# Signs of a gate group moved to the next even pair, its counts to the next odd one, and the last six row tiles reordered over two value buffers

## Chip, cores and metric

One core of a Trainium2 chip runs the kernel. The metric is the time of one execution on the device in microseconds (us), lower being better. Engines work in parallel, each on its own instructions in order: TensorE (PE; PEld is its weight load), VectorE (DVE), ScalarE (ACT), GpSimd (POOL) and SyncE (SP), which issues nearly all DMA transfers. Matrix products land in PSUM; everything else lies in SBUF.

## What is computed

Chunked attention, then a mixture of experts over its output. The reference, cut:

```python
# q, k, v: (8, 8, 576, 64); chunks of 64 rows
scores = scale * q_c @ k_c.T;  scores -= max(scores)
attn = exp(scores) / (sum(exp(scores)) + 1e-9)
x = (attn @ v_c)  ->  (4608, 512)
logits = x @ w_gate                       # 8 experts
expert_idx = argmax(logits);  probs = softmax(logits)
for e in range(8):                        # capacity 80
    tok = rows of expert e, the 80 with the largest gate weight if more
    out[tok] = gate_w[tok] * (relu(x[tok] @ w1[e]) @ w2[e])
```

Rows that no expert keeps are zero in the output. w1 and w2 of one expert are 2 MB each in float32.

## The kernel before

The 4608 rows are 36 row tiles of 128, worked in 18 pairs (loop at line 659). Pair n is spread over time: in iteration n TensorE computes `scores(n)`, transposes the probabilities of pair n-1 (`probs`, line 335), multiplies with the values of pair n-2 (`values`, tiles 2n-4 and 2n-3, line 355) and transposes the finished x of pair n-3 (`xtrans`, line 396). VectorE takes maxima, subtracts them (`minus`) and divides the values by their sums (`divide`, line 373). ScalarE takes the exponential of the transposed scores and copies transposed x out of PSUM. The values of a row tile go to one PSUM buffer, tag "o"; scores have another of the same size, tag "s", transposes a third, "tp". SP loads q, k and v, three pairs ahead, and stores x.

Four row tiles make a gate group T. In the odd ("due") pair 2T+5 `gate_mm` multiplies transposed x by w_gate, `gate_copy` brings the logits to SBUF and `gate_sum` transposes them back. `gate` (line 426) then puts a chain of small steps into the queue `gates`: maximum, shift, exponential, sum, one-hot of the best expert, a level from 1 to 256 made of the bits of the gate weight (`lb`, `bb`, `bo`), its inverse and the key with its three bf16 parts. `fill` takes the next step from the queue; the calls of `fill` are spread over the loop by hand and so set the place of each step. For rows below 32 the arithmetic of the level is on GpSimd.

The last queued steps are `count` and `left_add`. `count` has ScalarE compute, for each of the four row tiles, the sign of the level against 1 to 256 (`signs`, line 511); `left_add` has TensorE sum these per expert (`tally`, line 521) and VectorE subtract them from `left`, the capacity left at each level. With 14 queued steps before it, `count` comes up two pairs later, in the next odd pair, behind `gate_copy`, and `tally` before the values of the second tile:

```python
if rt < 28:
    queue.append((left_add, (rt, n)))
```

Behind the loop (line 704) the last row tiles are written out by hand: the probabilities of the last pair in two halves (`probs_last`), values 32 to 35, the last transposes and gate groups 7 and 8. `threshold` (line 551) finds each expert's smallest kept level. Rows above it are numbered, compacted with one-hot matrices (`hot`) and gathered. Weights of experts 0 and 1 come early, in eight parts (`early_weights`, from pair 15 on); parts 6 and 7 wait, through a small copy on GpSimd, for the last keyed levels `kb`. Behind them SP clears the first five of nine blocks of `out` and then loads the weights of experts 2 to 7 (line 863) as their buffers come free. The experts run six blocks of 128 slots on TensorE (`layer1`, line 183; `layer2`, line 215); the second block needs expert 2.

## Time and profile before

| | us |
|---|---|
| median of 3 runs | 288.51 |
| their range | 284.03 to 291.04 |
| the profiled execution | 285.64 |
| its span on the page | 283.8 |
| PE busy | 232.1 (82%) |
| PEld busy | 142.4 (50%) |
| DVE busy | 118.8 (42%) |
| ACT busy | 69.0 (24%) |
| POOL busy | 49.2 (17%) |
| DMA, mean rate | 299 GB/s of 84.80 MB |

Busy times are shares of the whole span; they average over stages that have different limits. A timeline row gives start, length, engine, line, operation, output from input, and in brackets the idle time just before and what ended it. "issue" is idle time for which the profile shows no cause.

### The profile page before, as it was taken

The numbers are of one execution on the slowest core, as the hardware profiler recorded it, in microseconds if no ns is written. First come the engines' busy times: TensorE is split into PE (matmuls) and PEld (weight loads), VectorE is DVE, ScalarE is ACT, GpSimd is POOL, SyncE is SP. The second block draws the span as 40 slices with busy tenths as digits, with TensorE's granted clock in tenths as the row PEclk, the third lists the DMA queues.
The fourth block names the chain that finished last, engine by engine and source line by source line (L and its number), as shares of the span: only waits on it lengthen the run. The fifth ranks groups of instructions, "written<-read, shape, count | busy, mean of one in ns | idle before, by whom it ended". The sixth has DMA issues, their size and how long they took to land. (4 is left out here: it accounts for less than half of the span.)

```text
span 283.8 us, 8481 instructions
## 1 busy us (share of the span) xinstructions
PE 232.1 (82%) x3697; PEld 142.4 (50%) x3697; DVE 118.8 (42%) x305; ACT 69.0 (24%) x120; POOL 49.2 (17%) x153
## 2 busy tenths in 40 slices
PE   8677888784889789785786794939999999999990
PEld 5556777673767677674564581303333332423320
DVE  4565778581656758384354872000020111111010
ACT  1121432524352434435243501102020010201000
POOL 5030003040221313040222737000000011010011
PEclk9797999998797979799689997977999999999997
DMA  7989999988497898476798599999999999992001
GB/s 267 381 272 389 345 352 383 349 267 302 128 329 245 276 309 271 139 275 247 233 290 285 185 362 411 413 415 393 410 406 402 413 404 407 413 404 112 3 35 32
DMA packets 35194, 84.80 MB, mean 299 GB/s; under 512 B 3472, under 2 KB 3600, under 8 KB 35152
## 3 DMA queue, kind: packets, MB, share of 16 engines
q1 hardware_dynamic: 33904, 80.72, 78.7%
q0 software_dynamic: 960, 2.88, 2.6%
q8 instruction: 31, 0.51, 0.7%
q10 hardware_dynamic: 288, 0.59, 0.5%
q14 instruction: 11, 0.09, 0.1%
HBM read 64.00 MB, written 20.45 MB: 298 GB/s over the span
## 5 line engine op out<-in xcount | busy, mean ns | idle before, releaser
L366 PE MATMUL o<-vb,pT 128*64 128x130 f32 x576 | 44.8, 301 | 11.4 <-issue 6.2
L190 PE MATMUL hc<-w,xtc 128*32 128x512 f32 x384 | 47.7, 632 | 4.5 <-DMA w<-in_w 4.4
L366 PEld LDWEIGHTS o<-vb,pT 128*64 128x64 f32 x576 | 35.4, 148 | 14.7 <-issue 8.7
L223 PE MATMUL yc<-w,htc 128*32 128x512 f32 x384 | 42.3, 592 | 0.0
L303 PE MATMUL s<-qk 64*64 64x64 f32 x1152 | 24.9, 239 | 6.3 <-issue 4.6
L190 PEld LDWEIGHTS hc<-w,xtc 128*32 128x32 f32 x384 | 12.4, 115 | 34.2 <-issue 28.4
L314 DVE TENSOR_REDUCE mx<-s 128x16 f32<-128x1024 f32 (+1 forms) x19 | 22.2, 1166 | 15.2 <-PE s L303 15.1
L340 ACT ACTIVATE pT<-pt 128x1024 f32<-128x1024 f32 x17 | 17.4, 1024 | 40.2 <-PE pt L331 40.2
L223 PEld LDWEIGHTS yc<-w,htc 128*32 128x32 f32 x384 | 12.4, 110 | 28.3 <-issue 28.3
L303 PEld LDWEIGHTS s<-qk 64*64 64x64 f32 x1152 | 21.8, 150 | 9.4 <-issue 6.3
L379 DVE TENSOR_TENSOR x<-o,rc 128x512 f32<-128x512 f32 x36 | 24.9, 691 | 1.2
L406 ACT COPY xT<-px 128x1024 f32<-128x1024 f32 x17 | 17.2, 1012 | 33.3 <-PE px L331 33.3
L229 POOL DMA_INDIRECT out<-ysc,si x6 | 6.0, 996 | 95.5 <-issue 49.7
L321 DVE TENSOR_TENSOR sm<-s,mx 128x1024 f32<-128x1024 f32 (+1 forms) x19 | 22.1, 1161 | 0.1
L195 ACT ACTIVATE hsc<-hc 128x512 f32<-128x512 f32 x6 | 3.6, 599 | 71.9 <-PE hc L190 71.9
L228 DVE TENSOR_SCALAR ysc<-yc,gatec 128x512 f32<-128x512 f32 x6 | 4.5, 751 | 33.0 <-PE yc L223 33.0
L212 DVE COPY htc<-hpc 128x512 f32<-128x512 f32 x6 | 4.2, 692 | 29.9 <-PE hpc L208 29.9
L490 POOL TENSOR_SCALAR u<-sx 128x4 f32<-128x4 f32 x8 | 1.6, 195 | 83.6 <-DVE sx L489 75.1
L538 PE MATMUL ph<-mine,lv 128*128 128x8 bf16 x72 | 7.1, 173 | 10.4 <-ACT lv L513 10.3
L331 PE MATMUL px<-ct,x 64*128 64x64 f32 x288 | 14.7, 251 | 0.9 <-ACT xT L406 0.9
L331 PEld LDWEIGHTS px<-ct,x 64*128 64x128 f32 x288 | 11.9, 158 | 4.7 <-issue 3.6
L197 DVE TENSOR_SCALAR hsc<-hc 128x512 f32<-128x512 f32 x6 | 4.2, 692 | 23.7 <-PE hc L190 23.7
(132 smaller groups left out, 235.5 us busy)
## 6 DMA issues: line engine op xcount, KB each, us to landing
w<-in_w SPq DMA_DIRECT2D x12, 2048.0 KB, 20.6
qk<-in_qk SPq DMA_DIRECT2D x35, 512.0 KB, 6.1
vb<-in_vv SPq DMA_DIRECT2D x72, 130.0 KB, 5.3
out<-zero SPq DMA_DIRECT2D x9, 1024.0 KB, 15.0
xs<-x SPq DMA_DIRECT2D x16, 512.0 KB, 5.8
w<-in_w SPq DMA_DIRECT2D x8, 1024.0 KB, 7.2
xs<-x SPq DMA_DIRECT2D x4, 256.0 KB, 4.2
qk<-in_qk ACTq DMA_DIRECT2D x1, 512.0 KB, 5.3
```

Source lines behind the costliest of these rows:

```text
L190: nc.tensor.matmul(h[o:o + 32, :], lhsT=xT[r][:, b, o:o + 32], rhs=getw(groups[r][g])[0][:, b, 512 * f:512 * f + 512], start=(b == 0), sto ...
L223: nc.tensor.matmul(y[o:o + 32, :], lhsT=hT[r][c // 4][:, c % 4, o:o + 32], rhs=getw(groups[r][g])[1][:, c, :], start=(c == 0), stop=(c == ...
L229: nc.gpsimd.indirect_dma_start(out=out, out_offset=bass.IndirectOffsetOnAxis(ap=si[:, r:r + 1], axis=0), in_=ys, in_offset=None, bounds_ch ...
L303: nc.tensor.matmul(ps[64 * u:64 * u + 64, h, c:c + 64], lhsT=t8[64 * h:64 * h + 64, 0, pr, u, :], rhs=t8[64 * h:64 * h + 64, 1, pr, u, :], ...
L314: nc.vector.tensor_reduce(d['mx'][:, :, c0:c1], d['s8'][:, :, c0:c1], axis=AX.X, op=ALU.max)
L321: nc.vector.tensor_tensor(d['sm'][:, c0:c1].rearrange("p c k h -> p h c k"), d['s8'][:, :, c0:c1], d['mx'][:, :, c0:c1, None].to_broadcast ...
L331: nc.tensor.transpose(pm[:, u, 64 * c:64 * c + 64], src(c)[rows], ident[rows, rows])
L340: nc.scalar.activation(d['pT'], pt, AF.Exp, scale=0.125)
L366: nc.tensor.matmul(po[64 * u:64 * u + 64, pr // 2, o:o + 130].rearrange("p (h x) -> p h x", h=2), lhsT=d['pT'][:, u, c:c + 64], rhs=v[:, : ...
L379: nc.vector.tensor_tensor(TT[T][:, r, :].rearrange("p (j m e) -> p j m e", j=2, m=4), pov[..., 0:64], rc[:, :, :, None].to_broadcast([P, 2 ...
L406: nc.scalar.copy(dst, pm)
L538: nc.tensor.matmul(ph[:, b, :], lhsT=U['lv', j][0][:, P * b:P * b + P], rhs=mine[:, j, :], start=not ab and rt != 24 and j == rt, stop=j = ...
```

## The change

- In the loop, the counts are no longer queued. In even pairs from 6 on the queue is emptied behind `xtrans`, and the four `signs` of the last group follow there. In odd pairs `tally` of the group before stands right behind `gate_copy`, and `left_add` (now the addition alone) behind the first divide. `gate_sum` comes behind the store of the pair instead of before `minus`; seven `fill`s follow instead of five.
- The chain is cut in three: `chain` to the level, `rest` (keyed level, sum plus 1e-9) and `late` (inverse, key). For the last three groups only `chain` is queued and the other parts are called by name; the keys are always GpSimd's.
- The counts of rows 24 to 27 come from comparisons on GpSimd (`steps_`), with a sum over the own rows 0 to 23 taken at the end of pair 16.
- The loop breaks off in the last pair. The last six row tiles follow in a new order, their values alternating between buffers "o" and "s"; maxima, subtraction and probabilities of the last pair are no longer in halves; the last x transpose uses "o", and the last gate takes the first pair's half first.
- Early weights 6 and 7 wait for the levels `bo`; 4 warming matmuls stand where 16 stood. Gate buffers are three deep instead of two.

```diff
         def gate_mm(T):
             pl = U['pl', T] = ps2.tile([P, P], F32, name=f"L{T}", tag="g")
-            for pr in range(4):
-                for j in range(4):
-                    xt = XT[2 * T + j // 2].rearrange("p c u j -> p c (u j)")
-                    nc.tensor.matmul(
-                        pl[32 * j:32 * j + 32], lhsT=wgp[:, pr], rhs=xt[:, 4 * (j % 2) + pr, :],
-                        start=pr == 0, stop=pr == 3, tile_position=(0, 32 * j))
+            order = [(pr, j) for pr in range(4) for j in range(4)]
+            if T == LG:
+                order.sort(key=lambda x: x[1] // 2)
+            for pr, j in order:
+                xt = XT[2 * T + j // 2].rearrange("p c u j -> p c (u j)")
+                nc.tensor.matmul(
+                    pl[32 * j:32 * j + 32], lhsT=wgp[:, pr], rhs=xt[:, 4 * (j % 2) + pr, :],
+                    start=pr == 0, stop=pr == 3, tile_position=(0, 32 * j))
...
             def key():
-                p.tensor_tensor(kk, oh, g[:, :, None].to_broadcast(bc), op=ALU.mult)
-                if rt >= 32:
-                    S['parts'] = parts
-                else:
-                    parts()
+                nc.gpsimd.tensor_tensor(kk, oh, g[:, :, None].to_broadcast(bc), op=ALU.mult)
+                parts()
...
-            def count():
-                if rt < 32:
-                    for j in range(rt, rt + n):
-                        signs(j)
-                else:
-                    signs(rt)
-                    for j in range(rt + 1, rt + n):
-                        steps_(nc.vector, j)
-
-            for fn in (
+            chain = [
                     lambda: v.tensor_reduce(m, lg, axis=AX.X, op=ALU.max),
                     shifted,
                     first,
@@ -492,21 +468,24 @@
                                             op=ALU.is_equal),
                     lambda: p.tensor_scalar(lb, u8.bitcast(I32), SHIFT, LOW + 1.0,
                                             op0=ALU.mult, op1=ALU.max),
-                    lambda: p.tensor_scalar(g, sx, 1e-9, None, op0=ALU.add),
                     level,
-                    lambda: v.reciprocal(g, g),
-                    lambda: p.tensor_scalar(bo[:, sl], bb, 2.0 ** -10, None, op0=ALU.add),
+                    lambda: p.tensor_scalar(bo[:, sl], bb, 2.0 ** -10, None, op0=ALU.add)]
+            rest = [
                     lambda: p.tensor_tensor(kb[:, :, sl].rearrange("p e r -> p r e"), oh,
                                             bb[:, :, None].to_broadcast(bc),
                                             op=ALU.mult),
-                    key,
-                    count):
-                if fn is count and rt == 28:
-                    S['signs'] = count
-                else:
-                    queue.append((fn, ()))
-            if rt < 28:
-                queue.append((left_add, (rt, n)))
+                    lambda: (v if rt == 24 else nc.gpsimd).tensor_scalar(
+                        g, sx, 1e-9, None, op0=ALU.add)]
+            late = [lambda: v.reciprocal(g, g), key]
+            for fn in chain + ([] if rt >= 24 else rest + late):
+                queue.append((fn, ()))
+            S['counts'] = [(signs, (j,)) for j in range(rt, rt + n)]
+            S["level", rt], S["sum", rt] = rest
+            S["inverse", rt], S["key", rt] = late
+
+        def rest(rt, *what):
+            for w in what:
+                S.pop((w, rt))()
...
-            if rt == 24:
-                cnt = gk.tile([P, NE], BF16, name="cnt", tag="cnt", bufs=1)
-                with nc.allow_low_precision(reason="whole numbers up to 28"):
-                    nc.vector.tensor_reduce(cnt, mine[:, 0:28, :].rearrange("p r e -> p e r"),
-                                            axis=AX.X, op=ALU.add)
             for b in range(2):
                 if rt == 24:
-                    nc.tensor.matmul(ph[:, b, :], lhsT=ones_b, rhs=cnt, start=True, stop=False)
...
-        def left_add(rt, n):
-            tally(rt, n)
+        def own_counts():
+            cnt = S['cnt'] = gk.tile([P, NE], BF16, name="cnt", tag="cnt", bufs=1)
+            with nc.allow_low_precision(reason="whole numbers up to 24"):
+                nc.vector.tensor_reduce(cnt, mine[:, 0:24, :].rearrange("p r e -> p e r"),
+                                        axis=AX.X, op=ALU.add)
+
+        def left_add(rt):
             if S.setdefault('first', rt) == rt:
                 nc.vector.tensor_scalar(left, U['ph', rt], -0.5, capt, op0=ALU.mult, op1=ALU.add)
...
+            rest(32, "level")
             with nc.allow_low_precision(reason="whole numbers up to 256"):
                 nc.vector.tensor_scalar(thr, pn, 1.0, None, op0=ALU.max)
...
                 if due:
                     gate_mm(T)
                     gate_copy(T)
-                maxima(n, 0, 4 if last else 8)
+                    if T >= 1:
+                        tally(4 * T - 4, 4)
+                maxima(n)
+                if last:
+                    minus(n)
+                    divide(2 * (n - 2))
+                    left_add(4 * T - 4)
+                    break
                 fill()
                 if n + NB < NPAIR:
                     for t in range(2):
                         load_qk(2 * (n + NB) + t)
                 if n >= 2:
                     divide(2 * (n - 2))
+                    if due and T >= 1:
+                        left_add(4 * T - 4)
                     fill()
                     values(2 * (n - 2) + 1)
                     if n - 2 + NBV // 2 < NPAIR:
                         load_v(2 * (n - 2) + 1 + NBV)
                 if n >= 3:
                     xtrans(n - 3)
-                if due:
-                    gate_sum(T, gates)
-                minus(n, 0, 4 if last else 8)
+                if n >= 6 and not due:
+                    flush(gates)
+                    for fn, args in S['counts']:
+                        fn(*args)
+                minus(n)
                 fill()
-                if last:
-                    maxima(n, 4, 8)
-                    minus(n, 4, 8)
                 if n >= 2:
                     divide(2 * (n - 2) + 1)
                     store(n - 2)
-                for j in range(5):
+                if due:
+                    gate_sum(T, gates)
+                for j in range(7):
                     fill()
+                if n == NPAIR - 2:
+                    own_counts()
                 for k in EARLY.get(n, ()):
                     early_weights(k)
-            n = NPAIR - 1
-            values(2 * n - 2)
-            probs_last(n, 0)
-            divide(2 * n - 2)
-            fill()
-            fill()
-            probs_last(n, 1)
-            values(2 * n - 1)
-            xtrans(n - 2)
-            divide(2 * n - 1)
-            store(n - 1)
-            for k in EARLY[NPAIR]:
+
+            def pops(k):
+                for j in range(k):
+                    fill()
+            values(31, "s")
+            probs(17)
+            gate_sum(6, gates)
+            values(32)
+            divide(31)
+            store(15)
+            for k in EARLY[17]:
                 early_weights(k)
-            values(2 * n)
+            pops(3)
+            values(33, "s")
+            xtrans(14)
+            divide(32)
+            pops(2)
+            values(34)
+            divide(33)
+            store(16)
+            for k in EARLY[18]:
+                early_weights(k)
             flush(gates)
-            values(2 * n + 1, "s")
+            for j in range(24, 28):
+                steps_(nc.gpsimd, j)
+            xtrans(15)
+            values(35, "s")
+            divide(34)
             gate_mm(7)
             gate_copy(7)
-            divide(2 * n)
-            xtrans(n - 1)
-            divide(2 * n + 1)
-            store(n)
-            for k in EARLY[NPAIR + 1]:
+            xtrans(16)
+            divide(35)
+            store(17)
+            for k in EARLY[19]:
                 early_weights(k)
             gate_sum(7, gates)
-            xtrans(n)
+            pops(2)
+            xtrans(17, "o")
             gate_mm(8)
+            flush(gates)
             gate_copy(8)
+            rest(24, "sum", "inverse")
+            signs(28)
+            signs(29)
+            gate_sum(8, gates)
+            tally(24, 4)
+            keep_warm(4)
+            pops(2)
+            rest(24, "level", "key")
+            signs(30)
+            signs(31)
+            left_add(24)
             flush(gates)
-            gate_sum(8, gates)
-            keep_warm(16)
-            fill()
-            fill()
-            S.pop('signs')()
+            signs(32)
+            for j in range(33, 36):
+                steps_(nc.vector, j)
             for k in (6, 7):
-                early_weights(k, kb[:, 0, 28 + 3 * (k - 6):29 + 3 * (k - 6)])
-            flush(gates)
-            S.pop('parts')()
+                early_weights(k, bo[:, 28 + 4 * (k - 6):29 + 4 * (k - 6)])
+            tally(28, 4)
+            left_add(28)
+            tally(32, 4)
+            rest(28, "level", "sum")
+            rest(32, "sum")
+            rest(28, "inverse", "key")
+            rest(32, "inverse", "key")
             for k in range(3):
                 clear(k)
-            left_add(28, 4)
-            tally(32, 4)
             keep_warm(1)
             threshold()
```

`maxima` and `minus` lose their column arguments, `halves` and `xtrans` gain a `tag`, `probs_last` goes, and the small gate tiles get `bufs=3`. `LG` is the last group, 8. `steps_` and `signs` are unchanged.

## Rows read from the trace of the kernel before

**Rows 1.** Windows by stage: length, engines' busy time, granted clock, DMA share, GB/s
```profile
34.00:39.95 5.95, 5.95 (x166) 4.97 (x162) 3.93 (x6) 2.40 (x4) 0.00 (x0) 1.00 0.95 316
46.63:125.03 78.40, 62.85 (x1490) 52.25 (x1486) 48.77 (x121) 30.64 (x50) 15.72 (x70) 0.89 0.79 262
125.03:158.45 33.42, 24.11 (x416) 18.72 (x413) 15.68 (x62) 13.38 (x27) 8.83 (x41) 0.90 0.76 258
158.45:174.44 15.99, 11.16 (x129) 8.70 (x127) 11.11 (x50) 2.33 (x8) 8.76 (x10) 0.99 0.95 345
174.44:189.59 15.15, 10.63 (x77) 3.36 (x77) 1.00 (x3) 1.88 (x4) 2.00 (x2) 0.84 1.04 414
189.59:283.80 94.21, 86.87 (x764) 29.39 (x764) 12.12 (x17) 8.73 (x15) 5.98 (x6) 0.95 0.76 297
```

**Rows 2.** Timeline, SP's clears and TensorE's wait for expert 2
```profile
158.75 10.07 SPq L593 DMA_DIRECT2D out<-zero  x5
...
189.59 6.06 PE L190 MATMUL hc<-w,xtc 128*32 128x512 f32 x28 [4.43 <-DMA w<-in_w]
```

**Rows 3.** Windows, first odd pair, sum of five odd, then of five even pairs
```profile
46.63:54.90 8.27, 6.82 (x174) 5.50 (x170) 4.25 (x8) 4.00 (x8) 1.71 (x8) 1.00 1.00 353
...
sum 48.22, PE 38.29 PEld 30.83 DVE 21.11 ACT 20.80 POOL 8.56; mean PE 7.66 PEld 6.17 DVE 4.22 ACT 4.16 POOL 1.71
...
sum 30.18, PE 24.56 PEld 21.42 DVE 27.66 ACT 9.84 POOL 7.16; mean PE 4.91 PEld 4.28 DVE 5.53 ACT 1.97 POOL 1.43
```

**Rows 4.** Timeline of one odd pair, from its scores to its second values
```profile
79.53 1.16 PE L303 MATMUL s<-qk 64*64 64x64 f32 x64
...
82.31 1.08 PE L413 MATMUL L<-xT,wgp 128*32 128x128 f32 x32
...
83.62 1.70 ACT L513 ACTIVATE lv<-io_b,bo 128x256 bf16<-128x256 bf16 x4
...
84.18 0.18 PE L538 MATMUL ph<-mine,lv 128*128 128x8 bf16 x1 [0.79 <-ACT lv L513]
...
85.38 0.29 PE L538 MATMUL ph<-mine,lv 128*128 128x8 bf16 x5 [0.22 <-ACT lv L513]
...
85.60 2.00 PE L366 MATMUL o<-vb,pT 128*64 128x130 f32 x16
```

**Rows 5.** Groups by line, ScalarE and VectorE: busy us, mean ns, idle before
```profile
L340 ACT ACTIVATE pT<-pt 128x1024 f32<-128x1024 f32 x17 | 17.4, 1024 | 40.2 <-PE pt L331 40.2
L406 ACT COPY xT<-px 128x1024 f32<-128x1024 f32 x17 | 17.2, 1012 | 33.3 <-PE px L331 33.3
...
L379 DVE TENSOR_TENSOR x<-o,rc 128x512 f32<-128x512 f32 x36 | 24.9, 691 | 1.2
L314 DVE TENSOR_REDUCE mx<-s 128x16 f32<-128x1024 f32 x17 | 20.8, 1223 | 14.7 <-PE s L303 14.6
L321 DVE TENSOR_TENSOR sm<-s,mx 128x1024 f32<-128x1024 f32 x17 | 20.7, 1217 | 0.1
L378 DVE RECIPROCAL rc<-rc 128x8 f32<-128x8 f32 x36 | 7.3, 203 | 1.2
L377 DVE TENSOR_SCALAR rc<-o 128x8 f32<-128x8 f32 x36 | 5.7, 160 | 7.0 <-PE o L366 6.4
```

**Rows 6.** Groups by line, GpSimd
```profile
L578 POOL TENSOR_SCALAR pk<-ct,ptok 128x128 bf16<-128x128 f32 x2 | 2.9, 1444 | 0.9 <-ACT ptok L770 0.9
...
L498 POOL TENSOR_SCALAR bo<-bb 128x4 f32<-128x4 bf16 x8 | 1.8, 230 | 0.7
```

**Rows 7.** Timeline, the last logits' transpose and the threshold
```profile
153.47 0.33 PE L423 MATMUL lT<-ct,lt 128*128 128x128 f32 x1 [0.37 <-ACT lt L419]
...
158.45 0.17 DVE L559 TENSOR_SCALAR thr<-pn 128x8 bf16<-128x8 f32 x1 [0.28 <-PE pn L557]
```

**Rows 8.** A stall of TensorE in the timeline, and the page's instruction queue
```profile
66.77 1.08 PE L413 MATMUL L<-xT,wgp 128*32 128x128 f32 x31 [2.73 <-issue]
...
q8 instruction: 31, 0.51, 0.7%
```

48 lines of the change are left out of this document (18 added, 30 removed).

## The prediction

> **What bounds the kernel now.** I read the stages first [rows 1]. From 189.59 us to the end TensorE is busy for 86.87 of 94.21 us while DMA has room (share 0.76), so that stage is a fixed tail. It can begin only when expert 2's first weight matrix has landed: TensorE waits 4.43 us for it at 189.59 [rows 2]. Ahead of that matrix in SP's queue stand five clears, issued from 158.75 on [rows 2]. DMA is full between the clears and the landing (share 0.95, then 1.04, 414 GB/s) [rows 1]. So the end follows when the clears are issued, and with them the last two early weights, which wait for the last gate values. That time is set by the attention loop and by the stretch behind its last pair, and there DMA has room: share 0.79 over ten pairs and 0.76 behind [rows 1].
>
> Inside the loop I compared the two kinds of pair [rows 3]. Five odd pairs, which hold a gate group, take 48.22 us together (9.64 each); five even ones take 30.18 (6.04 each). The timeline of one odd pair shows why [rows 4]: the gate matmuls run from 82.31 to 83.39, then TensorE waits for ScalarE's four signs (0.79 us before the first count matmul, then 0.22 before each), and the next values start only at 85.60, 2.21 us behind the gate. They then take 2.00 us; over the ten pairs the granted clock is 0.89 of full speed, against 1.00 in the pair at 34.00, which has a gate group but no counts yet [rows 1]. That pair takes 5.95 us. It is the nearest row there is for an odd pair whose counts find their signs ready.
>
> **The change part by part.** *Signs moved.* They leave the odd pair, where they stand behind the copy of the gate logits on ScalarE, and go behind the copy of x transposed in the even pair before. Four take 1.70 us [rows 4]. Behind them on ScalarE waits only the next pair's exponential. In an even pair ScalarE does one exponential (1.02), one copy (1.01) [rows 5] and now 1.70, together 3.7 of 6.04 us. The signs end about 2.7 us behind the start of their copy, and the next exponential has its input about 2.9 us behind the next scores (2.78 for scores, values and transpose up to the gate [rows 4]). So they hide, with little to spare; uncovered they would cost up to 1.7 us a pair. The level is ready by then: the flush in front of the signs only pulls forward small steps that GpSimd does at 0.23 us each [rows 6]. VectorE's reciprocal waits for six of these in a row, some 1.8 us, and VectorE is in the maxima and a divide meanwhile (1.22 and 0.69 + 0.20 + 0.16 [rows 5]).
>
> *Counts moved.* Eight matmuls now follow the gate with their signs long done. Five packed ones took 0.29 us [rows 4], so eight cost about 0.4. An odd pair becomes 5.95 + 0.4 = 6.35. VectorE's addition to `left` then waits until some 4.4 us into the pair, and `minus` ends at 5.8, before the next scores want the buffer at 6.3. I leave even pairs at 6.04. Ten pairs: 5 x 6.35 + 5 x 6.04 = 62.0 us instead of 78.40. DMA agrees on the bound: 0.79 x 78.40 = 61.9 us of full DMA [rows 1]. With both limits in one place I don't expect all of it. In one odd pair TensorE stood still for 2.73 us in the middle of the gate, waiting for nothing the profile shows [rows 8]; I allow one such stall again. Loop: 62.0 + 2.7 = 64.7, a gain of 13.7. The ends are 16.5 (no stall) and 8.2 (three).
>
> *The stretch behind the last pair.* Before, the last logits' transpose comes 28.4 us behind that pair's scores (153.47 - 125.03), the threshold 33.4 (158.45) [rows 7]; VectorE's split maxima and a single value buffer stretch it. After, two value buffers let TensorE go on: 2.78 to the gate, 1.08 gate, 0.4 counts, 4.3 in all. Then five values with five transposes: from the pair of 5.95, a values, a transpose and a logit transpose take 5.95 - 2.78 - 1.08 = 2.09, without the last part about 1.9; 5 x 1.9 = 9.5, and 1.08 for the next gate gives 14.8. VectorE has maxima, subtraction and six divides in that time, 1.22 + 1.22 + 6 x 1.05 = 8.7 us [rows 5], and two short gate chains; ScalarE two exponentials and three copies. Both fit. Half a copy, the second half of the reordered gate and the logit copy add about 2, so the last logits' transpose comes near 16.8 instead of 28.4: 11.6 earlier. From there to the threshold I leave 5.0 us. The exponential of the last group now queues behind two signs on ScalarE, and a reciprocal behind GpSimd's late sum, but fewer steps stand on the path. GpSimd's splitting of keys now falls behind the threshold, and its two one-hots (1.44 each [rows 6]) start about 0.6 later. Engines alone gain 11.0.
>
> DMA bounds this gain lower. From 125.03 to 189.59 the shares hold 0.76 x 33.42 + 0.95 x 15.99 + 1.04 x 15.15 = 56.4 us of full DMA in 64.56. At share 1.00 the gain is 8.2, at the 1.04 seen it is 10.3 [rows 1]. I take the middle, 9.3.
>
> *Steps on GpSimd.* Four comparisons of 256 columns go to GpSimd, and the next group's level chain queues behind them. They can start about 10.1 us behind the last scores, and that chain is wanted at 16.1, so up to 1.5 us each is free. No row has this size. Below, nothing is under 0.23, the small step; above, 128 columns took 1.44 beside busy VectorE, so 256 take at most 2.89 [rows 6]. I take about 0.7, nearer the small end: VectorE mostly reads PSUM in this stretch, while beside the 1.44 it compared two arrays in SBUF; that this matters is assumed. At 2.89 the chain is 5.6 us late: 10.1 + 11.6 - 16.1. The Trainium skill (GPSIMD Engine Reference, Performance versus the Vector engine) calls GpSimd the wrong engine for such work, at best 1.8 cycles an element, and says it shares SBUF ports with VectorE. By its figure 256 columns are an estimated 0.4 us, and the sum stays at 263; by the row, doubled, it is 268.6. The 1.44 is what its warning about ports would look like.
>
> *SP's queue.* Stores 15 to 17 and early weights 2 to 5 move forward with the divides; no v load is left behind the last pair to be passed. Early weights 6 and 7 now wait for the levels instead of GpSimd's keyed levels, about 2 us before the threshold instead of 1, and the clears queue right behind them. With DMA full this 1 us only fills the queue, so it is priced at nothing; if DMA idles there, it is a gain of 1.
>
> *Small edits.* The count over own rows (192 columns instead of 224) moves to the end of an even pair, where VectorE waits for scores. Deeper gate buffers cost nothing in time. The transposes of the last probabilities lose their half-and-half form, counted above. Twelve fewer warming matmuls may leave TensorE slower around the threshold; its granted clock behind the last pair is 0.90 already [rows 1]. I price it at 0 to 1.5 and keep 0.
>
> **Sum.** The profiled execution took 285.64 us, 283.8 of them span. 285.64 - 13.7 - 9.3 = 262.6, so 263. The median of the runs is 288.51, 1% above the profiled one; the same offset would make 265, inside the range.
>
> **Rivals.** *Better:* no stall and engines alone, 285.64 - 16.5 - 11.0 = 258, or less where DMA also packs closer; under 257 has chance 0.06. *GpSimd late:* 2.89 a step, 263 + 5.6 = 268.6, spread 264 to 273. Against it speaks what VectorE reads; for it, the only row of its kind. Chance 0.10. *Full DMA eats half:* at share 1.00 loads land later, two more stalls in the loop and none of the packing behind it, 263 + 5.5 + 5.8 = 274, spread 270 to 280. For it: the odd pair from 46.63, at share 1.00, moves only 353 GB/s [rows 3]. Chance 0.10. *The change does little:* if signs still end late for the counts, for instance because the level comes late, both halves shrink; 280 to 291, chance 0.08. GpSimd's level chain, five steps long, speaks against it.
>
> *Slower:* TensorE runs out of instructions. The 2.73 us stall has no releaser, and the trace has a queue for instructions (31 packets) [rows 8] on the DMA engines that I expect to be full. Each stall costs 2.73. Eight or nine eat the gain of 23; from eleven on ((23 + 5.7)/2.73) the kernel is slower by over 2%. One in every pair and three behind the loop, less the one counted, give 263 + 12 x 2.73 = 296. Against it: the pair from 46.63 ran at share 1.00 with granted clock 1.00 in 8.27 us [rows 3], hardly more than the 6.35 and the 2 us of the signs' wait. Chance 0.04. The Trainium skill (Runtime: NRT & Kernel Launch, Instruction fetch mechanics) says that an engine refills its instruction memory in 16 KiB blocks over a DMA queue of its own and that this is mostly hidden; the single stall fits "mostly".
>
> **Chances.** The forecast, 257 to 269, has 0.62. Range 255 to 277: the forecast, GpSimd late, about half of the better case and most of the half-eaten one, 0.8. About 2% is what a measurement tells from no change here, 280 and 291. Faster: 0.62 + 0.06 + 0.10 + 0.10 = 0.88; within 2%: 0.08; slower: 0.04.
>
> **What would show it.** Odd pairs near 6.4 us with the count matmuls packed in one run and no wait for signs; granted clock near 1.00 in the loop; DMA share near 1.0 from the loop to the landing; the last logits' transpose some 17 us and the threshold some 22 us behind the last scores; TensorE still waiting for expert 2's matrix. Wrong if signs push the exponential, if GpSimd's comparisons take over 1.5 us, if unexplained stalls multiply, or if TensorE reaches the experts later than the matrix.

## The result, and the profile after

The changed kernel takes 264.05 us (median of 4 runs, 262.08 to 266.81) beside 286.27 us for the kernel before in the same comparison (283.35 to 291.04): ratio 0.9285, 95% interval 0.9184 to 0.9385. The ratio leaves out executions that took over 1.5% longer than the shortest of the same kernel. The forecast was 263. The sum behind it is less exact than its end. The profiled execution of after is the longest of its four, 266.81 us with a span of 265.0, so its parts add up to 265.0 and not to the median:

| step, us | before | forecast | after |
|---|---|---|---|
| to the scores of the eighth pair | 46.63 | 46.6 | 48.24 |
| ten pairs | 78.40 | 64.7 | 70.94 |
| last scores to expert 2's first matmul | 64.56 | 55.3 | 54.16 |
| expert 2 to the end | 94.21 | 94.2 | 91.66 |
| span | 283.8 | 260.8 | 265.0 |

The ten pairs gave 7.5 us, not 13.7. The stretch behind them gave 10.4 against 9.3. The experts gave 2.5 that nobody had counted, and 1.6 us were lost ahead of the first of the ten pairs. Most of that last term is the kind of stall taken up below: this execution has two there, of 0.83 and 1.27 us, the one before has one of 1.01. Four other executions with the same work up to there begin the ten pairs at 46.0 to 46.9. The ten pairs of this execution are not unusual: in the five kernels below that change neither the loop's order nor its loads they took 69.8 to 72.0 us in the profiled execution.

The stages of after, in the columns of [rows 1]: length, busy time of the engines, granted clock, DMA share, GB/s.

```profile
35.50:41.41 5.91, 5.08 (x116) 4.08 (x107) 4.05 (x8) 1.60 (x4) 0.00 (x0) 1.00 1.04 386
48.24:119.18 70.94, 58.19 (x1489) 48.78 (x1486) 49.38 (x121) 30.36 (x50) 15.74 (x71) 0.95 0.87 288
119.18:141.52 22.34, 19.14 (x412) 15.72 (x409) 15.36 (x57) 11.62 (x22) 10.09 (x31) 1.00 0.96 331
141.52:160.76 19.24, 13.66 (x129) 10.37 (x127) 11.12 (x50) 2.33 (x8) 10.79 (x20) 0.80 1.05 409
160.76:173.34 12.58, 12.09 (x76) 3.59 (x77) 1.00 (x3) 1.88 (x4) 2.00 (x2) 0.77 1.04 411
173.34:265.00 91.66, 84.44 (x764) 29.01 (x764) 12.12 (x17) 8.71 (x15) 5.97 (x6) 0.98 0.78 304
```

In the ten pairs the clock rose from 0.89 to 0.95 and the DMA share from 0.79 to 0.87. The fourth row, from the threshold to the first gathered rows' transposes, is the one that got longer: 19.24 us at clock 0.80, where before had 15.99 at 0.99.

The odd pairs at 78.90, 62.63 and 90.95, the sum of five odd ones and the sum of five even ones, as in [rows 3]:

```profile
78.90:84.91 6.01, 6.01 (x173) 5.12 (x169) 4.54 (x10) 4.00 (x8) 0.32 (x2) 1.00 0.95 322
62.63:72.35 9.72, 7.79 (x174) 6.52 (x170) 4.81 (x10) 4.05 (x8) 0.00 (x0) 0.82 0.89 306
90.95:101.99 11.04, 7.81 (x173) 6.45 (x169) 5.15 (x10) 4.03 (x8) 0.32 (x2) 0.85 0.90 309
...
sum 41.74, PE 34.46 PEld 28.67 DVE 23.95 ACT 20.10 POOL 1.29; mean PE 6.89 PEld 5.73 DVE 4.79 ACT 4.02 POOL 0.26
...
sum 29.20, PE 23.73 PEld 20.11 DVE 25.43 ACT 10.26 POOL 14.45; mean PE 4.75 PEld 4.02 DVE 5.09 ACT 2.05 POOL 2.89
```

An odd pair that nothing disturbs takes 6.01 us (the forecast was 6.35) and TensorE is busy for all of it. Two others take 9.72 and 11.04 for the same work.

The timeline of the undisturbed pair, against [rows 4]: start, length, engine, line.

```profile
79.92 1.70 ACT L492 ACTIVATE lv<-io_b,bo 128x256 bf16<-128x256 bf16 x4
...
81.68 1.08 PE L401 MATMUL L<-xT,wgp 128*32 128x128 f32 x32
81.85 1.02 ACT L338 ACTIVATE pT<-pt 128x1024 f32<-128x1024 f32 x1 [0.23 <-PE pt L329]
82.69 0.36 PE L512 MATMUL ph<-mine,lv 128*128 128x8 bf16 x8
82.98 1.11 PE L351 MATMUL o<-vb,pT 128*64 128x130 f32 x16
```

The signs run from 79.92 to 81.62 and are done 1.07 us ahead of the counts. The exponential behind them still waits 0.23 us for its own input, so they don't push it. All eight counts run in 0.36 us without a wait, and the second values follow 1.30 us behind the gate's start instead of 3.29. They take 1.11 us, not 2.00.

Behind the last pair, against [rows 7] and [rows 2]: the last logits' transpose, the threshold, SP's clears and expert 2's first matmuls.

```profile
137.68 0.33 PE L411 MATMUL lT<-ct,lt 128*128 128x128 f32 x1 [0.36 <-ACT lt L407]
...
141.52 0.17 DVE L539 TENSOR_SCALAR thr<-pn 128x8 bf16<-128x8 f32 x1
```

```profile
140.66 12.94 SPq L573 DMA_DIRECT2D out<-zero  x5
...
173.34 3.63 PE L191 MATMUL hc<-w,xtc 128*32 128x512 f32 x28 [0.46 <-DMA w<-in_w]
```

The transpose comes 18.5 us behind the last scores (forecast 16.8, before 28.4) and the threshold 22.3 (forecast 21.8, before 33.4). TensorE now waits 0.46 us for expert 2's matrix instead of 4.43, and its next 28 matmuls take 3.63 us instead of 6.06 [rows 2]. The difference, 2.43 us, is nearly all of the 2.55 that the experts gave.

GpSimd's groups, against [rows 6]: the new comparisons and its two one-hots.

```profile
L497 POOL TENSOR_SCALAR lv<-io_b,bo 128x256 bf16<-128x256 bf16 x4 | 4.5, 1162 | 0.1
...
L558 POOL TENSOR_SCALAR pk<-ct,ptok 128x128 bf16<-128x128 f32 x2 | 1.2, 606 | 0.0
```

And what did not come out: TensorE's stalls. One of them in the timeline, in the pair at 62.63, against [rows 8]:

```profile
65.41 0.30 PE L401 MATMUL L<-xT,wgp 128*32 128x128 f32 x1
67.64 1.93 PE L401 MATMUL L<-xT,wgp 128*32 128x128 f32 x31 [1.93 <-issue]
69.50 0.37 PE L512 MATMUL ph<-mine,lv 128*128 128x8 bf16 x8
69.80 1.72 PE L351 MATMUL o<-vb,pT 128*64 128x130 f32 x16
```

TensorE does one matmul of the gate, stands still for 1.93 us, and then does the rest at a lower clock: 31 matmuls in 1.93 us, where the pair above takes 1.08 for 32. Such a stall has no cause in the profile; seven stand in the ten pairs (0.44, 1.63, 1.93, 1.05, 0.51, 1.02, 2.20 us), 8.78 us in all.

### The profile page after: what moved, and what is told of

Same layout as the page of the kernel before. It is cut to its first block, busy times and chain, and to the rows that moved or that the text cites. A ratio compares the mean times of both kernels' runs of the same rounds, so it can differ in the third digit from the quotient of the medians.

```text
span 265.0 us, 8465 instructions
## 1 busy us (share of the span) xinstructions
PE 223.7 (84%) x3693; PEld 137.4 (52%) x3693; DVE 119.3 (45%) x302; ACT 66.8 (25%) x115; POOL 53.8 (20%) x158
## 5 line engine op out<-in xcount | busy, mean ns | idle before, releaser
L351 PE MATMUL o<-vb,pT 128*64 128x130 f32 x576 | 42.7, 290 | 8.4 <-PE pt L329 5.3
L191 PE MATMUL hc<-w,xtc 128*32 128x512 f32 x384 | 46.8, 621 | 0.5 <-DMA w<-in_w 0.5
L351 PEld LDWEIGHTS o<-vb,pT 128*64 128x64 f32 x576 | 33.6, 142 | 11.6 <-PE pt L329 5.1
L314 DVE TENSOR_REDUCE mx<-s 128x16 f32<-128x1024 f32 x18 | 22.0, 1224 | 22.3 <-PE s L304 22.2
L304 PEld LDWEIGHTS s<-qk 64*64 64x64 f32 x1152 | 21.0, 141 | 15.6 <-issue 11.4
L338 ACT ACTIVATE pT<-pt 128x1024 f32<-128x1024 f32 x18 | 18.4, 1025 | 41.9 <-PE pt L329 41.9
L319 DVE TENSOR_TENSOR sm<-s,mx 128x1024 f32<-128x1024 f32 x18 | 21.9, 1214 | 0.1
L229 DVE TENSOR_SCALAR ysc<-yc,gatec 128x512 f32<-128x512 f32 x6 | 4.5, 751 | 33.4 <-PE yc L224 33.4
L401 PE MATMUL L<-xT,wgp 128*32 128x128 f32 x288 | 12.1, 291 | 2.3 <-issue 1.9
L329 PE MATMUL pt<-ct,sm 64*128 64x64 f32 x288 | 13.7, 237 | 0.0
L329 PE MATMUL px<-ct,x 64*128 64x64 f32 x288 | 13.2, 234 | 0.1
```

The lines of the kernel that those rows point to most:

```text
L191: nc.tensor.matmul(h[o:o + 32, :], lhsT=xT[r][:, b, o:o + 32], rhs=getw(groups[r][g])[0][:, b, 512 * f:512 * f + 512], start=(b == 0), sto ...
L304: nc.tensor.matmul(ps[64 * u:64 * u + 64, h, c:c + 64], lhsT=t8[64 * h:64 * h + 64, 0, pr, u, :], rhs=t8[64 * h:64 * h + 64, 1, pr, u, :], ...
L314: nc.vector.tensor_reduce(d['mx'], d['s8'], axis=AX.X, op=ALU.max)
L319: nc.vector.tensor_tensor(d['sm'].rearrange("p c k h -> p h c k"), d['s8'], d['mx'][:, :, :, None].to_broadcast([P, 2, 8, 64]), op=ALU.sub ...
L329: nc.tensor.transpose(pm[:, u, 64 * c:64 * c + 64], src(c)[rows], ident[rows, rows])
L338: nc.scalar.activation(d['pT'], pt, AF.Exp, scale=0.125)
```

## The experiments

**What the stalls depend on: DMA.** The loop's loads were cut in both kernels; all instructions of the engines stay. In the changed kernel, and in the same way in the one before:

```
-            d = QKV["qk", i] = wk.tile([P, QK], F32, name=f"qk{i}", tag="qk", bufs=2 * NB)
-            eng.dma_start(d, qk[i // 2, i % 2])
+            j, w = i % (2 * NB), QK if i < 2 * NB else QK // 2
+            if i < 2 * NB:
+                QKV["b", j] = wk.tile([P, QK], F32, name=f"qk{j}", tag=f"qk{j}", bufs=1)
+            d = QKV["qk", i] = QKV["b", j]
+            eng.dma_start(d[:, 0:w], qk[i // 2, i % 2, :, 0:w])
...
-            for h in range(2):
+            for h in range(2 if i < NBV else 1):
```

> The changed kernel loading, from the seventh row tile on, only the q half of each q and k tile and only one of the two value halves; the rest keeps older data, so 0.8 of 2.1 MB a pair is not moved and the output is not the reference's. My theory (the stalls without a releaser are instruction blocks that come late because DMA is nearly full): they shrink from 8.8 us to under 3 in the ten pairs, which take 62 to 65 us. Rival 1 (the block is late whatever else DMA carries): stalls stay near 8 us, ten pairs near 70. Rival 2 (the loop waits for q and k data): the pairs fall below 62 us.

> The kernel before with the loads of the loop cut: from the ninth row tile on only half of q and k is loaded, and of the values only one of two halves from the seventh on; its output is therefore not the reference's. The same cut in the changed kernel gave ten pairs of 60.06 us with stalls of 1.55. Theory (the counts' wait for their signs is an engine matter, and stalls of instruction fetch are a matter of full DMA): the ten pairs fall from 78.40 only by the stalls, of which there are 6.7 us, to 70 to 75 us; the waits of 0.8 + 3 x 0.22 us for signs and a granted clock near 0.9 remain; the edge of the changed loop grows from 7.5 to 10 to 14 us, near the 13.7 forecast. Rival (before was bound by DMA too, and the signs' wait was only where it showed): ten pairs near 62, no edge left.

The changed kernel with fewer loads: the window of the ten pairs, and TensorE's waits in it (line, what for, total, times, longest).

```profile
42.34:102.40 60.06, 54.07 (x1489) 45.82 (x1486) 48.82 (x121) 30.68 (x50) 15.63 (x71) 1.00 0.67 220
...
PE L L404 <- issue: 1.2, 2, 0.9
PE s L307 <- issue: 0.4, 1, 0.4
```

The same of the kernel before with fewer loads.

```profile
42.93:116.15 73.22, 60.11 (x1489) 50.08 (x1485) 48.77 (x121) 30.65 (x50) 15.72 (x70) 0.93 0.54 176
...
PE ph L541 <- ACT lv L516: 7.2, 20, 0.8
```

With the DMA engines at 0.67 instead of 0.87 the stalls of the changed loop shrink from 8.78 to 1.55 us, the clock stays at 1.00 and the ten pairs take 60.06. The loop before keeps its 20 waits for signs, 7.2 us, at a share of 0.54. The edge of the new loop is then 73.22 - 60.06 = 13.2 us, close to the 13.7 of the forecast. Each of the two kernels ran once. Three more stops of some 1.15 us in the loop before, also without a cause in its profile, stand just behind a divide and stay at a share of 0.54 (3.4 us in three), so they are not of this kind. The full loads take 10.9 us from the new loop (70.94 - 60.06) and 5.2 from the old one (78.40 - 73.22). The rival, that before was bound by DMA too, falls. The changed loop fell below the 62 us that were to speak for waits on q and k. But in its full version no wait of TensorE is put down to q or k, and 70.94 less 7.23 us of stalls and the 3.59 us of slow clock reckoned below is 60.1: the fall needs no such wait.

**What the stalls are: borders in the stream of instructions.** Sixteen more warming matmuls early in the kernel shift everything behind them.

```
                 if n == 1:
-                    warm_up(8)
+                    warm_up(24)
```

> The changed kernel with 24 instead of 8 warming matmuls in pair 1, which is 16 matmuls (and weight loads) more ahead of everything that follows, and 1.7 us at most. Theory (TensorE stands still at the borders of instruction blocks when DMA is full): each stall of the loop comes 16 matmuls earlier in the order of instructions than in the changed kernel. Behind 19 score matmuls of a pair becomes behind 3, behind the first gate matmul becomes behind the 15th matmul ahead of it, and so on; the packets of 16,384 B land at about the same times. Rival (the stalls sit at certain operations, the gate's or the scores' data): they stay behind the same matmuls. Total 264 to 267 us.

Here is the same stretch of TensorE's timeline in this kernel.

```profile
63.47 0.27 PE L329 MATMUL pt<-ct,sm 64*128 64x64 f32 x1
65.15 0.65 PE L329 MATMUL pt<-ct,sm 64*128 64x64 f32 x15 [1.40 <-issue]
65.73 1.08 PE L401 MATMUL L<-xT,wgp 128*32 128x128 f32 x32
```

The stall that came behind the first gate matmul comes behind the first of the 16 transposes ahead of the gate, 16 matmuls earlier. Numbering TensorE's matmuls from the first score, and taking, from number 574 on, the stops of over 0.3 us that end 0.9 to 1.9 us behind the landing of a packet of the instruction queue (31 packets, 0.51 MB on the page, 16,384 B each in the trace), gives this, worked out from the traces (length of the stop in us, - where there is none):

```
matmul no.   after   16 matmuls ahead   loads spread   rows 32-35 last
574          0.83    0.51               1.05           0.35
700          1.27    0.74               1.29           -
825          0.44    0.56               -              -
951/952      1.63    1.25               -              1.36
1077/1078    -       1.74               0.69           1.24
1203         1.93    1.40               1.38           -
1330         1.05    1.07               1.80           -
1455         -       -                  -              0.63
1581         0.51    1.01               0.36           1.16
1706         1.02    -                  -              0.48
1833         2.20    3.31               1.84           2.74
2084         -       -                  0.32           -
2211         -       0.46               1.18           -
2336         1.08    0.99               1.64           1.91
2462         -       2.76               0.80           1.35
```

The places are the same numbers in every kernel, about 125.9 matmuls apart ((2336 - 574)/14), whatever instruction stands there. Matmul and weight load together are two instructions, so a step of 251.7 instructions for a packet of 16,384 B is 65 B an instruction. TensorE stands still where its next block of instructions has not come. Nothing at these places in the program is slow by itself. The time in all was 268.04 us in one run, 1 us over what was expected.

**The move of the signs.** All stays as changed, but the signs go back behind the copy of the gate logits, the counts right behind them.

```
                     gate_copy(T)
                     if T >= 1:
+                        for fn, args in S['counts']:
+                            fn(*args)
                         tally(4 * T - 4, 4)
...
-                    for fn, args in S['counts']:
-                        fn(*args)
```

> The changed kernel with the four signs back in the odd pair, behind the copy of the gate logits, and the counts right behind them; all else stays. Theory (the move of the signs is what shortens the loop): in each of five odd pairs the eight counts wait again for ScalarE, 0.8 + 3 x 0.22 us and more, 1.6 to 2.2 us a pair, 8 to 11 in ten pairs; part of it is given back, because DMA is then less full and stalls of instruction fetch shrink from 8.8 us: ten pairs 75 to 80 us instead of 70.9, 268 to 275 us in all. Rival (DMA sets the loop's time, share 0.95, and the wait would be hidden): ten pairs 71 to 73, 264 to 266 us.

It took 271.94 us (269.62 to 275.14), ratio to before 0.9508 (0.9400 to 0.9616). The window of the ten pairs and TensorE's first wait in it:

```profile
47.69:126.53 78.84, 62.40 (x1490) 51.67 (x1486) 49.52 (x121) 30.33 (x50) 15.74 (x71) 0.89 0.78 261
...
PE ph L512 <- ACT lv L492: 7.2, 20, 0.8
```

The loop is back at 78.84 us (before 78.40), with the same 20 waits of 7.2 us and the same clock of 0.89. The gain of the loop comes from where the signs stand; the loop's other edits, which this kernel keeps, don't shorten it alone. The two loops differ in stalls at block borders, though: three of 5.98 us here against one of 2.73 before. Without them they would take 72.9 and 75.7, so up to 2.8 us from the other edits are not excluded.

**The halves apart.** First only the loop's part on the kernel before, then only the stretch behind the last pair on the old loop. Core of the first diff, against before:

```
+                    if T >= 1:
+                        tally(4 * T - 4, 4)
...
-                if due:
+                if n >= 6 and not due:
+                    flush(gates)
+                    for fn, args in S['counts']:
+                        fn(*args)
+                if last:
                     gate_sum(T, gates)
```

> The loop of the changed kernel (signs behind the transposed copy in even pairs, counts packed behind the gate in odd ones) with the old stretch behind the last pair. My theory (loop and tail are separate gains; instruction fetch takes part of the loop's back): ten pairs from the eighth scores on take about 70 us instead of 78, with count matmuls packed and several stalls of TensorE without a releaser of 0.5 to 2 us; the stretch behind the last scores stays near 64 us up to the experts' wait for their matrix; the whole is 6 to 9 us faster than before, near 279. Rival (full DMA is the bound and the tail gain only came from DMA packed closer): the loop gets shorter by as much, but the wait for expert 2's matrix grows by the same amount, and the whole stays within 2 us of before.

It took 275.92 us (275.13 to 281.78), ratio 0.972 (0.956 to 0.988). The window of the ten pairs:

```profile
47.63:119.33 71.70, 56.42 (x1490) 47.60 (x1486) 49.02 (x121) 30.52 (x50) 15.67 (x71) 0.98 0.85 288
```

Core of the second diff, against the changed kernel:

```
+            if rt < 24:
+                queue.append((lambda: [signs(j) for j in range(rt, rt + n)], ()))
+                queue.append((lambda: (tally(rt, n), left_add(rt)), ()))
...
-                    if T >= 1:
-                        tally(4 * T - 4, 4)
```

> The old loop (signs and counts from the queue in odd pairs) with the new order behind the last pair. My theory: the loop keeps its 78 us; from the last scores to the first matmul on expert 2 about 54 us instead of 64.6, and the experts about 2 us shorter as in the changed kernel; the whole 11 to 14 us faster than before, near 273. Rival (the tail's gain comes from the loop having filled or emptied DMA): the tail gains under 6 us.

It took 273.93 us (269.59 to 277.11), ratio 0.969 (0.954 to 0.984). The windows of the ten pairs and from the last scores to the threshold:

```profile
46.32:121.49 75.17, 61.57 (x1490) 51.29 (x1486) 48.90 (x121) 30.58 (x50) 15.79 (x70) 0.91 0.82 276
121.49:144.49 23.00, 19.54 (x412) 15.75 (x409) 15.52 (x58) 11.61 (x22) 11.43 (x37) 0.98 0.88 321
```

Beside 285.91 us for the kernel before in that comparison the halves gain 10.0 and 12.0 us, together 22.0; the whole change gained 22.2 (286.27 - 264.05). That they add is not shown: the ratios give 2.8 and 3.1% against 7.15%, with intervals of 1.6, 1.5 and 1.0 either way, and in the profiled executions the halves overlap. From the last scores to expert 2 the loop's half alone gains 4.4 us, the other alone 9.9, both 10.4; in the ten pairs it is 6.7, 3.2 and 7.5. Neither the 4.4 nor the 3.2 was expected. The loop's half brings the old threshold from 33.4 to 29.0 us behind the last scores, and leaves the wait for expert 2's matrix at 4.48 us: the matrix lands 60.1 us behind the last scores, since the clears still follow the old threshold.

**The second value buffer.** The last row tiles keep their new order but share one buffer:

```
-            values(31, "s")
+            values(31)
...
-            values(33, "s")
+            values(33)
...
-            values(35, "s")
+            values(35)
```

> The changed kernel with one value buffer for the last six row tiles instead of two; the order of the work stays. Theory (the tail was stretched by the single buffer and by the order together): each of three values waits for the divide of the one ahead, 1.05 us, less what transposes fill; the last logits' transpose comes 19.5 to 22 us behind the last scores instead of 18.5. The end moves by less than that, 0 to 2 us, because expert 2's matrix waits for a full DMA queue anyway (TensorE waited 0.46 us for it): 264 to 267 us. Rival (the second buffer carries the tail's gain): transpose 24 us or more behind, 268 us or more.

It took 267.35 us (264.29 to 267.70), ratio 0.9345 (0.9226 to 0.9465). The last logits' transpose comes 20.9 us behind the last scores and the threshold 24.8, 2.4 us later each than with two buffers, as expected. The profile with two buffers has a stall of 1.08 us in this stretch and this one has none, so the buffer is worth 2.4 to 3.5 us at the threshold; the values wait 3.6 us here and not at all there. In the total, which is 0.35 us over what was expected, the interval overlaps that of the changed kernel, and what arrives at the end is not resolved.

**The longer compaction.** The stage behind the threshold grew by 3.3 us. My first explanation was the shorter warming of TensorE.

```
             tally(24, 4)
-            keep_warm(4)
+            keep_warm(16)
```

> The changed kernel with 16 instead of 4 warming matmuls in front of the last gate values. My theory: the granted clock between threshold and experts returns from 0.80 to near 1.00, that stretch shrinks from 19.2 to 16 to 17 us, but TensorE then waits 2 to 3 us for expert 2's matrix instead of 0.46, so the whole stays within 1 us of the changed kernel. Rival (TensorE, not DMA, sets the experts' start): the whole gains 2 to 3 us.

It took 263.71 us (260.04 to 271.61), the same as the changed kernel. The stage took 18.87 us where 16 to 17 were expected, 0.4 less than in the changed kernel. TensorE's timeline there shows why:

```profile
141.71 0.67 PE L796 MATMUL two<-comp,pk 128*128 128x40 bf16 x8
142.22 0.27 PE L567 MATMUL pwarm<-io_b,ones_b 128*128 128x256 bf16 x1
143.96 0.68 PE L796 MATMUL two<-comp,pk 128*128 128x40 bf16 x9 [1.47 <-POOL comp L454]
...
146.43 1.83 PE L831 MATMUL kr<-ct,kc 128*128 128x128 f32 x8
```

The clock now holds up to 142.2, and then TensorE waits 1.47 us for GpSimd. In the changed kernel GpSimd splits the keys of rows 28 to 35 only behind the counts, from 141.0 to 147.4 us, around and behind the threshold. There VectorE compares its one-hots from 143.96 on, and a step that takes 0.21 to 0.25 us elsewhere takes 0.57 to 0.70 (changed kernel):

```profile
143.06 0.25 POOL L453 TENSOR_TENSOR r<-r,comp 128x32 f32<-128x32 f32 x1
...
144.80 0.70 POOL L451 TENSOR_TENSOR r<-keys,comp 128x32 f32<-128x32 f32 x1
145.57 0.69 POOL L452 CAST comp<-r 128x32 bf16<-128x32 f32 x1
146.34 0.57 POOL L453 TENSOR_TENSOR r<-r,comp 128x32 f32<-128x32 f32 x1
```

Row 32 stands fourteenth in the compaction's order, so 22 other matmuls queue behind its key. The next kernel takes rows 32 to 35 last and gives GpSimd no one-hots:

```
-            for rt, way in ((31, "p"), (32, "a"), (33, "a"), (34, "a"), (35, "p")):
+            for rt, way in ((32, "a"), (33, "a"), (34, "a"), (35, "a")):
...
-            for b0, n in ((0, 5), (5, 8), (13, 8), (21, 6), (27, 4)):
+            for b0, n in ((0, 5), (5, 8), (13, 8), (21, 6), (27, 5)):
...
-            order = [*range(0, 13), 32, *range(13, 21), 33, 31, *range(21, 27), 34, 35,
-                     *range(27, 31)]
+            order = list(range(RT))
```

> The changed kernel, but the 36 matmuls that compact the rows take rows 32 to 35 last, and the one-hots of rows 31 and 35 are built on VectorE and ScalarE instead of GpSimd. Theory (the stage from threshold to the offsets is 3.3 us longer than before because GpSimd splits the keys of rows 28 to 35 only behind the threshold, 141.2 to 147.4, beside VectorE's one-hot comparisons that slow it from 0.21 to 0.7 us a step, so that TensorE waits 0.86 us at row 32 and falls to the lower clock, at which transposes and warming matmuls take 1.84 and 1.91 instead of 1.08 and 1.04): no wait for GpSimd is left or under 0.4 us, threshold to summed candidates 6.3 to 6.8 us instead of 7.68 (before 6.28), and, where the clock stays up, candidates to the first indices 2.4 instead of 3.97; the whole stage 16.0 to 17.5 us. With the four warming matmuls the clock may still fall ahead of it (0.75 at 141.5 to 144.0), which leaves 0.8 to 1.6 of the loss. Rival (the stage is longer because DMA is full, share 1.05 against 0.95): 19 us as in the changed kernel.

Threshold to offsets (the sum into `si`), first the changed kernel, then this one:

```profile
141.52:157.83 16.31, 13.66 (x128) 10.36 (x126) 10.73 (x48) 2.33 (x8) 8.74 (x18) 0.79 1.05 409
```

```profile
141.54:155.32 13.78, 12.05 (x128) 9.47 (x126) 10.92 (x48) 2.93 (x10) 7.64 (x16) 0.88 1.03 388
```

Before took 13.31 between the same points. So 2.5 of the 3.0 us are back, at nearly the same DMA share, which speaks against DMA as the cause. (With the loads of the loop cut the stretch had stayed at 16.37, but its share there was still 1.02, so that run says nothing of it.) Yet the total, 267.4 us in one run, is no better. What follows in this kernel:

```profile
172.17 5.32 PE L191 MATMUL hc<-w,xtc 128*32 128x512 f32 x28 [2.35 <-DMA w<-in_w]
```

From the threshold on TensorE is 3.1 us earlier, but the threshold itself comes 24.5 us behind the last scores instead of 22.3, because stalls of 1.91 and 1.35 us stand there instead of one of 1.08. So TensorE is ready for expert 2 only 0.9 us earlier, 52.8 us behind the last scores, and waits 2.35 us for its matrix, which lands at 55.1 (after: 54.2). Behind the wait the clock is lower, 0.67, and 28 matmuls take 5.32 us instead of 3.63. The gain became a wait, because the matrix came no sooner.

**Versions that should beat both.** One issues the second of a pair's q and k loads behind the second values:

```
-                    for t in range(2):
-                        load_qk(2 * (n + NB) + t)
+                    load_qk(2 * (n + NB))
...
+                if n + NB < NPAIR:
+                    load_qk(2 * (n + NB) + 1)
```

> The changed kernel, but the second of a pair's two q and k loads is issued behind the second values instead of together with the first. Theory (instruction blocks come late because every load in flight fills the DMA engines): if the bursts matter, fewer or shorter stalls, ten pairs 66 to 69 us instead of 70.9 and 260 to 263 us in all. If it is the mean load that counts (share 0.95), nothing moves: 70 to 72 and 264 us. Rival (the later loads become late themselves): scores wait for their q and k, ten pairs over 73, above 266 us.

It took 263.97 us (262.74 to 264.88), ratio 0.9313 (0.9212 to 0.9413). Its profile has ten pairs of 68.06 us with stalls of 7.57, but the median does not move. The same loads in the last kernel of this section gave ten pairs of 74.39 us with stalls of 11.6, so the 68.06 is chance more than an effect; whether bursts or the mean load count is not shown. (The share of 0.95 in this expectation and in that of the signs is the granted clock of its row; DMA's share is 0.87.) Then the tail, on top of rows 32 to 35 last:

```
-            keep_warm(4)
+            keep_warm(16)
...
-            for k in range(3, 5):
-                clear(k)
...
-                    for n in range(5, NT):
+                    for n in range(3, NT):
                         clear(n, nc.sync)
```

> The changed kernel with rows 32 to 35 last in the compaction and no one-hots on GpSimd, as in the run before (threshold to offsets 13.8 instead of 16.3 us), with 16 instead of 4 warming matmuls, and with two of the five clears (1 MB each) moved behind expert 2's weights. Theory (behind the last pair, transfers and TensorE now arrive at expert 2 together, so that neither alone gives anything; the last run showed it for TensorE, which then waited 2.35 us and ran 28 matmuls in 5.32 us instead of 3.63): expert 2's matrix lands about 5 us earlier, TensorE comes to it without a wait 50.5 to 52.5 us behind the last scores instead of 54.16, and 261 to 263 us in all. Rival (DMA was not the limit, the experts' stage takes up what the stage before gives): 264 us.

> The same with the second of a pair's q and k loads issued behind the second values, as in the run that did this alone (ten pairs 68.1 us, 263.97 us in all). Theory: the loop's gain of 0 to 2.9 us adds to the tail's, 259 to 262 us. Rival (the loop's spread is chance, a matter of which instruction blocks come late): the same as the tail alone.

The first took 263.72 us (260.86 to 269.71), ratio 0.9195 (0.9104 to 0.9286), the second 262.50 (259.87 to 267.90), ratio 0.9172 (0.9086 to 0.9258). Both intervals overlap that of the changed kernel: if there is a gain, it is about 1%, and these runs don't show it. In the profile of the first, its longest run, the stage did what was meant (threshold to offsets 13.57 us at clock 1.00, no wait for expert 2's matrix). But there TensorE stood 2.4 us for instructions behind the last pair, waited 5.0 instead of 4.1 us for the first gathered rows, and came to expert 2 54.7 us behind the last scores instead of 50.5 to 52.5. It then waited 1.5 us for expert 5's second matrix; in the second kernel it came at 52.3 and waited 1.9 us there, so part of what the moved clears gave came back as a later wait. Whether these would be gone in a run near the median is open.

## Why the prediction was right, and where it was not

**What bounds it, and the move of the signs: right.** With the signs back, the loop was back at 78.84 us. An undisturbed odd pair took 6.01 where 6.35 was predicted, and even pairs without their two stalls took 27.64/5 = 5.53 where 6.04 was left standing. The signs did not push the next exponential, with 0.23 us to spare.

**The loop's size: wrong, in one term.** "I allow one such stall again", 2.73 us, is the step that failed. There were seven, 8.78 us, and the two longest each drew a slow stretch behind them: the pair at 62.63 took 9.72, which is 6.01 and the stall of 1.93 and 1.78 more; the pair at 90.95 took 11.04, which is 6.01, stalls of 3.22, and 1.81 more. Starting from the loop with few loads, 60.06 + (8.78 - 1.55) + 1.78 + 1.81 = 70.88, and 70.94 was measured. Against the 64.7 that is 6.05 us more of stalls and 3.59 of slow clock, less 1.70 and 2.56 because odd and even pairs are shorter than priced, and 0.9 not placed: 6.2. The direction could have been seen: a stall that depends on how full DMA is was carried over, at the number and price it had at a share of 0.79, into a loop planned to fill DMA. The bound from DMA itself was right: 0.87 x 70.94 = 61.7 us of full DMA, forecast 61.9.

The rival for this was *TensorE runs out of instructions*, and it named the right mechanism with the wrong weight: it reckoned in stalls of 2.73, and seven of 1.25 on average came. What spoke against it, one pair at share 1.00 without a stall, was one pair of ten. Of the four signs of being wrong this one came true, unexplained stalls multiplied, and two signs of being right failed with it: the loop's clock was 0.95 and its DMA share 0.87, both forecast near 1.0. The rule cited there from the Trainium skill (Runtime: NRT & Kernel Launch, Instruction fetch mechanics), refills in blocks of 16 KiB over a queue of their own, agrees with the 31 packets of 16,384 B. "Mostly hidden" agrees with 1.55 us of stalls at a share of 0.67 and not with 8.78 at 0.87.

**The stretch behind the last pair: right, and for the DMA bound's reason.** The engines' part was 18.5 and 22.3 us where 16.8 and 21.8 were predicted; 1.08 of the former is one stall. Of the 9.9 us by which the last transpose comes earlier, the second buffer gives 2.4 to 3.5; the loop's half alone brings 4.5 of them, and what the new order gives by itself no run separates. The middle between DMA's 8.2 and 10.3 was taken, and 10.4 was measured: 0.96 x 22.34 + 1.05 x 19.24 + 1.04 x 12.58 = 54.7 us of full DMA fill the 54.16. That DMA sets this end is what the kernel with rows 32 to 35 last bears out: what TensorE got back became a wait, and its 55.1 us hold 0.98 x 55.1 = 54.0 us of full DMA. But TensorE is ready only 0.46 us before the matrix in the changed kernel, so both limits stand in one place: with two clears moved away it waits for nothing at expert 2 and still comes at 54.7 and 52.3. In the rival *Full DMA eats half* the 5.8 us behind the loop have no working.

**Steps on GpSimd: right.** Four comparisons took 1.16 us each, between the 0.7 taken and the limit of 1.5. They ended at 134.96 and the next group's chain began at 136.07, so they cost nothing; I didn't try them on VectorE. The estimate of 0.4 us from the Trainium skill (GPSIMD Engine Reference, Performance versus the Vector engine) is too low by a factor of nearly three here.

**GpSimd's splitting of keys: wrong, without a price.** "Its two one-hots start about 0.6 later" was the whole account; they started 5.86 us behind the threshold, before at 2.71. The split keys of row 32 came at 147.4, 5.9 us behind the threshold, and the stage grew by 3.3 us, about 2.5 of it from there; the warming, priced at 0 to 1.5, gave 0.4 where it was put back alone. It stayed nearly without effect because expert 2's matrix landed no sooner.

**The experts: not foreseen.** They were called a fixed tail. 2.43 of their 94.21 us were the slow clock behind the wait of 4.43, and left with it.

The profiled run missed the sum by 4.2 us: 6.2 too few in the loop and 1.6 ahead of it, less 1.1 behind it and 2.5 from the experts. That the median is within 1.1 us of 263 is luck: 2.5 us of the experts that were not foreseen, 1.1 us behind the loop, and a median 2.8 us below the profiled run cover most of the loop's miss.

## What to carry to other kernels

Price a wait that grows with the load of another resource at the load that the change will make: a single occurrence at today's load says little of how many will come. A stage that ends on a transfer has two clocks; shortening the engines' side and the transfers' side must be planned together, or the gain becomes a wait. What is moved off the path on an engine's queue is due somewhere: look up its first reader and how many instructions stand behind that reader.

## What the runs showed of the hardware

- TensorE stands still at the borders of its instruction blocks when DMA is full, in the four kernels of the table for 0.32 to 3.31 us, at the same numbers of the matmul stream, and goes on 1.2 to 1.6 us behind the landing of a 16,384 B packet. At a DMA share of 0.67 ten pairs lost 1.55 us in this way, at 0.79 (before) one stop of 2.73, and at 0.87 the changed kernel lost 8.78. The share alone doesn't give the size: the kernel with the signs back lost 5.98 at 0.78, the loop's half alone 11.8 at 0.85.
- A stop of TensorE costs more than its length when the clock falls behind it. In the changed loop the granted clock was 1.00 behind a stop of 1.63 us (55.27 to 56.93), 0.64 behind one of 1.93 (67.64 to 72.35) and 0.53, nearly the lower level of 1.2 GHz throughout, behind one of 2.20 (98.49 to 101.99). The length alone doesn't decide it: at expert 2 a wait of 1.93 us cost nothing more. There the same 28 matmuls took, by the wait ahead of them in ten kernels:

```
wait, us          0.46  1.09  1.47  1.72  1.93  1.96  2.35  4.43  4.48  4.51
28 matmuls, us    3.63  3.63  3.63  3.63  3.63  3.63  5.32  6.06  6.07  6.08
```

- A step of GpSimd's splitting of keys (32 columns) takes 0.21 to 0.25 us elsewhere and up to 0.7 beside VectorE's comparisons of two SBUF arrays. That these cause it is read from the times alone. The two one-hots of 128 columns that took 1.44 us each before took 0.61 behind those comparisons [rows 6].
